# A new operation list for a gated convolution and a gated MLP on one core, with a small load moved to the front

## The chip, the cores and the metric

The kernel runs on one core of a Trainium2 chip. The metric is the device time in microseconds from the first to the last instruction of the program. The engines of the core are TensorE (PE, matmuls; its weight loads are shown apart as PEld), VectorE (DVE), ScalarE (ACT), GpSimd (POOL) and SyncE (SP), which only issues transfers here. They run side by side and wait for one another through semaphores.

## The reference

One block of 2048 positions (S) and 640 channels (D). A vector `c` gives six modulation rows. The first part is a layer norm, a short convolution of `k` over four positions, a product with `v`, a long convolution over the whole sequence through a Fourier transform, and a product with the normalised input. The second part is a gated MLP whose gate is mixed over positions. Batch 1, bfloat16:

```python
mod = (silu(c) @ w_mod).reshape(1, 6, 1, -1)           # sa, ca, ga, sb, cb, gb
h = layernorm(x) * (1 + ca) + sa                       # x is A_q
k_shift = sum over t of k_pad[:, t:t+S] * shift_k[:, 3-t]
kv = k_shift * v
y = irfft(rfft(kv, 2S) * rfft(ssm_k, 2S))[:S] + kv * ssm_D
x = x + ga * (h * y)
h = layernorm(x) * (1 + cb) + sb
z = gelu(h @ w_in)                                     # 640 -> 1728
z1, z2 = z[:, :864], layernorm(z[:, 864:])
g = w_sp @ z2 + b_sp[:, None]                          # 2048 x 2048 over positions
x = x + gb * ((z1 * g) @ w_out)
```

## The kernel before

The long convolution is done as two short transforms on TensorE. The channels are cut into five blocks (`u`) of 128. For each block, stage 1 turns the filter (XK) and the signal (XU) with a small table F1, `forward` turns the result with M2 in eight steps (`st`) of two frequencies, VectorE multiplies signal and filter, `inv` turns back with G2, and a last transform with the table E gives y. D is added to the filter's first tap, so that `kv * ssm_D` needs no work of its own.

The kernel records its first half (everything up to the mixing over positions) as about a thousand operations with their dependencies, and then issues them in the order of a written list. Each token names the engine (P, A, D, G, S for PE, ACT, DVE, POOL, SP) and the number of the operation:

```python
ORDER = """
D13 G96 D12 D122 D7 D8 D9 S14 A0 S5 A4 D95 D97 D104 A1 D110 D105 A2 G125 D6 S77 S78 ...
"""
def run(self, engines):
    order = [(x[0], int(x[1:])) for x in ORDER.split()]
    ...
    for e, i in order:
        o = self.ops[i]
        assert e in o["eng"] and done.issuperset(o["deps"]), (e, i)
        o["fn"](engines[e])
```

Within one engine the list is the order of execution; between engines only the dependencies order. An operation that may run on several engines is placed by its letter. These are the operations that the prediction speaks of:

```python
# loads, tables and D
nc.gpsimd.memset(D_col[:], 0.0)                        # at the end of GpSimd's set-up
op("SAG", "ldc", ... dma_start(c_bf, c), w=["c"])
op("A", "silut", activation(warm, warm, Silu)); op("A", "silu", activation(sc, c_bf, Silu))
op("A", "sint", activation(warm, warm, Sin), r=["silu"], w=["sint"])
op("SAG", "ldD", ... dma_start(D_col[0:P:16, :], d_fft), w=["D"])      # 8 x 80 elements
op("D", "addD", ... tensor_tensor(XK[:, x:y, 0], XK[:, x:y, 0], D_col[...], op=ALU.add), r=["D"], w=[XK])
op("A", "f1c", cosine(f1c, f1i), r=["f1a", "sint"])     # the table F1
op("D", "f1m", tensor_tensor(F1bd, f1c, gmask, op=ALU.mult), r=["f1c", "f1g"], w=["F1"])
# k and v by transposing loads, taps, kv to DRAM and back
op("S", "ldk", dma_start_transpose(kv[...], A_k or A_v))
op("P", "taps", 4 matmuls of 128x512 per quarter);  op("D", "tv", tensor_tensor(v, taps, v, op=ALU.mult))
op("SA", "kvw", dma_start(kv_scr, v));  op("SA", "ldX", dma_start(XU, kv_scr))
# one step of a block
op("P", "fwd", 6 matmuls);  op("D", "prod", tensor_tensor(T, pu, KH, op=ALU.mult))      # pu lies in PSUM
op("GD", "csum", tensor_tensor(W, T0, T1, op=ALU.add or ALU.subtract))                 # 2 inputs in SBUF
op("P", "inv", 6 or 12 matmuls); op("AD", "zc", copy(Z, pz))
# modulation and residual, per block and group of 4 x 128 positions
op("GD", "ghm", tensor_tensor(gh, gh, gca1 or gsa, op=ALU.mult or ALU.add))             # 2 inputs in SBUF
op("D", "ym", tensor_tensor(gh, gh, y, op=ALU.mult))                                     # y lies in PSUM
op("GD", "res", tensor_tensor(xt, xt, gh, op=ALU.add));  op("D", "ln2", bn_stats(st2, xt))
# second norm, per group; group 0 is flipped on TensorE, the others by a transposing move
op("G", "rstd2", rstd_from_var(...));  op("D", "nmr2", scalar_tensor_tensor(nmr2, mv2, -1, rstd2, ...))
op("DA", "zx", tensor_scalar(xn2, xt, mv2, rstd2, ...) or activation(...))
op("P", "hfl", transposes); op("AD", "hmod", ...)      # group 0
op("S", "turn", dma_start_transpose(hT, xn2)); op("DA", "hmod2", ...)                    # groups 1 to 3
op("P", "zz", 5 matmuls of 128x432); op("A", "gelu", ...)                                # 64 of these
op("P", "fill", k matmuls of the identity, results unused), k in FILLS
```

After the list the second half runs in program order: for each of 16 row blocks 32 matmuls that mix over positions (line 945 of the kernel before), a product on VectorE (948), a transposing move, and 14 matmuls with `w_out` (963).

Of the kernel before, what the change touches and what calls it, by code (L numbers as in the profile page):

```python
# [9 lines left out]
ACT = mybir.ActivationFunctionType  # L10
# [5 lines left out]
P = 128  # L16
# [17 lines left out]
FILLS = (4, 4, 4, 1, 2, 4, 2, 1, 4, 2, 2, )  # L34
# [6 lines left out]
D13 G96 D12 D122 D7 D8 D9 S14 A0 S5 A4 D95 D97 D104 A1 D110 D105 A2 G125 D6 S77 S78 D111 D81 A3 A106 A10 D11 A18 P1020  # L41
P1021 P1022 P140 P1023 P21 D116 D117 A107 S16 D82 P19 D98 A141 A118 A142 A119 D99 A100 D22 P143 A145 D144 S15 A101
A112 S17 A113 P146 A147 A148 G108 S29 S508 G109 D20 S27 D102 P1024 P25 D26 G120 A121 P23 D24 A28 P149 G114 A150 G115
P128 D129 D103 P1025 P131 D132 P134 A151 P158 G31 A159 D135 P162 A163 D512 P137 S30 G130 D138 D513 D514 D139 P164 A165
P156 A157 P154 A155 P36 D37 S79 P160 A161 P152 A153 P32 D33 G136 P168 P171 G43 A170 S80 D169 P34 D515 S83 A173 A172
P177 A179 P174 A176 D35 D178 P38 D39 D85 P166 A175 P194 D195 A167 G133 P220 A221 P180 G196 P204 A123 P222 A223 S509
D181 D205 P190 D191 P182 P214 G197 A516 G206 D183 P224 A225 P198 G55 A517 A199 S41 P184 P46 P226 A227 G207 P208 A209
S40 D215 G216 P48 D185 G186 G217 D518 S42 P200 G187 P192 A519 P230 A231 P218 G126 D201 D47 D520 P210 D211 S84 P244
A245 D49 P50 D51 A219 G521 D522 P240 D193 A241 P246 A247 D534 P232 A233 S550 P44 P228 A229 P250 A251 P242 A243 D535
D536 P551 A552 P238 A239 P248 A249 D45 S511 D527 D537 P234 A235 P553 P236 A237 S86 D538 D539 D88 P292 D528 P256 D257  # L50
P276 D277 G278 S510 A293 A529 G279 P212 A213 P294 A295 P252 A554 S52 D253 P188 A189 D523 P282 P202 P298 A299 D283 G258
G259 P266 A203 P254 A255 P296 A297 D267 D524 A530 P280 A281 S555 P556 P284 G268 G269 P558 D557 G597 D525 D526 S87 P316
A317 P310 P262 D531 P260 S53 S54 D263 D559 A311 P318 D285 S560 G532 A540 D541 D533 G576 P302 A303 P58 P286 A319 P60
A546 D287 D547 G288 D59 D578 P300 A301 G289 D61 P264 A542 A261 D543 D548 P312 A313 P320 A321 P304 A305 D544 P561 P56
D562 D579 D577 S89 P306 A307 D91 P322 A323 D545 G580 D57 P62 D63 P308 A309 P314 A315 P364 D549 D124 D582 P324 D325
P270 P338 D339 A365 P563 A265 G67 P366 P334 D335 A271 S584 P326 S64 A367 P368 G581 G583 P585 D564 D586 P358 P272 G340
G341 P290 G598 A369 G655 D359 G360 P587 S65 D588 A327 D273 P370 P342 G361 P348 D349 A291 D350 P589 D636 P72 A371 P376
D590 A377 D638 P274 A343 A275 S90 P388 A389 S66 P328 D329 P362 G603 D604 D657 G692 P372 A373 G330 D73 P591 D592 P390
G595 A391 P336 A337 P354 D355 P378 P392 A363 P70 A379 A393 P74 P374 P344 A375 P394 A395 D71 P384 D75 G351 D599 S92 D94
G600 D345 D634 D601 G602 S605 P68 D69 A385 P386 A387 P396 D397 P436 A437 P400 P352 A353 D401 P606 D607 G593 P382 A383  # L60
S76 G661 D635 P356 A357 P426 D427 G331 P440 A441 P608 P346 A347 D609 P380 A381 S565 G402 G403 S93 D637 P442 A443 D696
G697 G640 G641 P610 D611 P406 D407 P332 A333 P420 P438 A439 D421 P612 D613 P398 P404 A399 D594 P454 A455 D614 P460
P416 D693 P428 G422 G423 D616 A461 D417 P430 D431 A429 P466 A467 P566 A567 P410 A405 G659 P458 A459 P462 D694 A463
P418 S642 G619 D411 D639 D622 P444 A445 D618 D419 G432 P464 A465 G433 P643 D644 D623 D621 P448 A449 P450 A451 P424
A425 D620 P645 D646 P482 G662 P434 A435 P468 P647 P408 D483 S568 A409 P452 A453 D469 D648 G412 G413 P414 G484 G485
P502 D503 P492 D493 A415 P649 P470 A471 G656 P488 S738 P569 G624 P456 A457 P486 D489 A487 D650 P446 D617 P498 D499
G494 A447 G495 P496 A497 P478 D479 P490 A491 G504 G505 P472 P500 A501 P480 A481 G660 G658 S663 P664 P506 A570 A507
D473 D474 D475 P476 G698 A477 D665 P666 D667 P1026 P704 P668 G699 D615 G651 P706 D669 P1027 P670 A705 D707 D671 P702
P700 D701 A703 S571 P572 A573 D672 D674 G695 D673 P708 D709 D710 D713 D712 D711 D741 D740 G742 P724 D725 P717 D718
A127 P574 A575 P731 D743 A744 D745 P1028 P750 D714 P746 A747 G653 D732 D751 D719 P1029 P748 P754 D749 P752 A755 G677  # L70
D676 D753 P1030 P775 D716 S739 D715 D675 D757 D756 P800 D721 G652 D720 P772 D679 A776 G758 P806 D681 P782 D678 D759
A760 D723 D822 D823 D722 D680 A807 D761 D825 D824 G826 P768 D769 A801 P762 D763 A773 D827 D828 D829 D831 A783 D830
P802 P764 D726 D654 D730 D784 D682 D685 D683 A765 D684 G687 P766 A767 D728 P804 P770 A771 A805 P779 A780 A803 D729
P810 A811 P786 A787 D781 S832 P793 A794 P808 A809 P796 D691 A797 D690 D727 D626 A834 P789 A790 D836 D837 P814 P812
A835 D833 P862 G596 P838 A813 D688 G629 A815 A839 P880 D627 A881 P859 A860 A863 D777 P852 A853 P845 A846 D628 P874
A875 P848 A849 D890 D625 D888 D889 P876 A877 D686 D891 G892 D893 D894 D897 D896 D689 D895 P841 D631 A842 P868 A869
D733 P870 P878 D633 A871 S898 D630 D847 D737 D734 A900 P872 A879 D736 D632 D861 D956 D954 A873 P866 A901 P855 D843
A856 D840 A867 D844 D903 D774 D778 D902 D735 D955 D899 D957 D850 P914 P932 A933 P904 A905 A915 G958 D959 A960 D961
D962 D791 P934 D788 D795 D963 S964 A935 P918 A919 D792 P936 A937 D798 P907 A908 D851 D854 D799 D857 D858 D785 G816
D817 A820 P928 A929 D819 P911 A912 P925 D906 D818 A965 D967 A926 P921 A922 P942 P940 A941 D968 D969 D966 P970 P1002  # L80
P980 D864 A943 D916 A971 P938 A1003 D909 D913 D917 D865 A981 D920 P984 D930 D982 D910 D927 D931 P977 D923 A821 A939
A978 D979 A985 D986 P1004 A1005 D924 P987 A988 P991 A992 D989 G882 P998 G948 D949 D950 A952 P994 A995 D883 D953 P973
A886 A974 P1010 D972 D884 P1000 A999 A1001 A887 P1012 A1013 D885 D993 D951 A1011 D975 D976 P1008 P1006 A1007 D996 D997
P946 D983 D990 G1014 D1015 A947 D1017 P944 A945 A1019 D1018 A1009 D1016
"""


class Plan:


    def __init__(self):
        self.ops, self.touch = [], {}

    def op(self, eng, kind, fn, r=(), w=(), new=(), n=1):

# [28 lines left out]
def kernel(  # L124
# [20 lines left out]
    nc = tc.nc  # L145
    _, S, D = A_q.shape
# [58 lines left out]
    with ExitStack() as actx:  # L205
# [25 lines left out]
        op = plan.op  # L231
# [16 lines left out]
        def cosine(e, dst, turns64):  # L248

            e.activation(dst, turns64, ACT.Sin, bias=mpi[:], scale=TWO_PI / 64.0)  # L250
# [762 lines left out]
```

## Time and profile before

| | before |
|---|---|
| time, median of the runs | 334.87 us |
| profiled execution: span | 332.8 us |
| TensorE busy | 314.2 us (94%), 2596 instructions |
| VectorE busy | 218.8 us (66%), 466 |
| ScalarE busy | 147.0 us (44%), 257 |
| GpSimd busy | 93.5 us (28%), 120 |
| first matmul of the mixing | at 203.9 us |

One of the three runs before took 1839 us; the median leaves it out of account. In the slices of busy time (each digit a fortieth of the span, in tenths) one sees the two halves. VectorE is at 9 through the first half and at 2 or 3 in the second, TensorE is at 9 from the fourth slice on but for two slices at 8 and one at 5 at the end:

```profile
## 2 busy tenths in 40 slices
PE   6699999999999998699999899999999999999995
PEld 1366789778789897554455455555555555555553
DVE  6579999999999998989876783262223222233323
ACT  2476999896778756366667676000000000000010
POOL 2251733659489695551111111000000000000000
PEclk9699999999999999999999999999999999999999
```

PEclk is the clock that TensorE was granted. A matmul's busy time contains time in the pipeline, so a 9 of PE does not say that TensorE is the limit; which engine is, has to be read from the gaps and from the chain of waits. In the lists of operations, "out<-in" names the tiles, then come the shapes, the count and the busy time; `big` holds k and v (and later `w_in`), `X` the filter or signal, `gh` the modulated input and then the product with y, `xt` the running x, `Z` the inverse transform and later the normalised input, `s`, `sm`, `pu`, `pz` are tiles in PSUM.

### The profile page before, as it was taken

To read this page: it belongs to the slowest core of one execution; us is meant where nothing else is said; L and a number is where in the kernel's file an instruction comes from. 1 tells how busy PE (TensorE), PEld (TensorE's weight loads), DVE (VectorE), ACT (ScalarE), POOL (GpSimd) and SP (SyncE) were. 2 spreads that over 40 slices of the span, in tenths; PEclk is the share of its full clock that TensorE was granted. 3 is DMA by queue.
4 is the path that set the end of the run, shared out by engine and by line. 5 is a ranking of instruction groups with operands and counts; after the bars stand their busy time and mean duration, and the time that the engine had idled before them with its cause. 6 is when DMAs were issued, how large, how long until landed. Compare 5 with 4: busy or idle time off the path is not lost.

```text
span 332.8 us, 6423 instructions
## 1 busy us (share of the span) xinstructions
PE 314.2 (94%) x2596; PEld 206.7 (62%) x2603; DVE 218.8 (66%) x466; ACT 147.0 (44%) x257; POOL 93.5 (28%) x120
## 2 busy tenths in 40 slices
PE   6699999999999998699999899999999999999995
PEld 1366789778789897554455455555555555555553
DVE  6579999999999998989876783262223222233323
ACT  2476999896778756366667676000000000000010
POOL 2251733659489695551111111000000000000000
PEclk9699999999999999999999999999999999999999
DMA  7969999989969876004134991455557666422221
GB/s 128 204 129 249 243 299 239 234 186 194 197 185 156 272 131 231 2 1 79 21 60 81 175 226 51 91 118 116 116 131 131 135 83 150 110 49 47 49 47 59
DMA packets 128580, 44.99 MB, mean 135 GB/s; under 512 B 117704, under 2 KB 127784, under 8 KB 128552
## 3 DMA queue, kind: packets, MB, share of 16 engines
q1 hardware_dynamic: 127104, 44.33, 60.9%
q10 hardware_dynamic: 1448, 0.26, 0.4%
q8 instruction: 20, 0.33, 0.4%
q14 instruction: 8, 0.07, 0.1%
HBM read 16.11 MB, written 5.24 MB: 64 GB/s over the span
## 4 chain that ended last, share of the span: by engine, by line
PE 74%; DVE 14%; DMA 6%; issue 2%; ACT 2%; ACTq 0%; DVEq 0%
PE ps L945 28%; PE pu L240 15%; PE pz L240 12%; PE po L963 9%; PE sm L240 6%; DMA Z<-Z 4%; DVE Tf L456 3%; PE s L240 3%; DVE T L456 2%; DMA D_col<-in_A_ssm_D_dram 2%; DMA big<-in_A_k_dram 1%; DVE gh L648 1%; DVE W L465 1%; DVE st L569 1%; DVE big L542 1%
## 5 line engine op out<-in xcount | busy, mean ns | idle before, releaser
L945 PE MATMUL ps<-X,wT 128*128 128x432 bf16 x512 | 95.7, 346 | 0.0
L945 PEld LDWEIGHTS <-wT 128*128 128x128 bf16 x512 | 50.1, 98 | 42.2
L956 ACT COPY uT<-pt 128x896 bf16<-128x896 bf16 x1 | 0.9, 905 | 117.5 <-PE pt L955 117.5
L240 PEld LDWEIGHTS <-Z 128*128 128x128 bf16 x320 | 31.0, 98 | 29.4 <-ACT Z L858 1.7
L240 PE MATMUL pu<-X,M 128*128 128x128 bf16 (+1 forms) x480 | 46.2, 237 | 1.7 <-DVE Tf L456 1.1
L240 PEld LDWEIGHTS <-M 128*128 128x128 bf16 x480 | 37.5, 98 | 8.3 <-issue 3.0
L948 DVE SCALAR_TENSOR_TENSOR u<-ps,bcol,G 128x432 bf16<-128x432 f32 x18 | 12.0, 668 | 42.2 <-PE ps L945 42.2
L465 POOL TENSOR_TENSOR W<-Tf 128x256 bf16<-128x256 f32 x37 | 27.4, 760 | 27.7 <-DVE Tf L456 26.1
L243 ACT CAST X<-s 128x1024 bf16<-128x1024 f32 x32 | 32.8, 1024 | 4.5 <-PE s L240 4.4
L240 PE MATMUL pu<-big,Z 128*128 128x432 bf16 x160 | 32.3, 346 | 1.1 <-ACT X L883 1.1
L240 PE MATMUL pz<-big,Z 128*128 128x432 bf16 x160 | 32.3, 346 | 0.9 <-ACT X L883 0.7
L963 PE MATMUL po<-w_o,uT 128*128 128x320 bf16 (+1 forms) x224 | 32.8, 299 | 0.0
L948 DVE SCALAR_TENSOR_TENSOR u<-ps,bcol,M 128x432 bf16<-128x432 f32 x14 | 9.3, 667 | 30.9 <-PE ps L945 30.9
L240 PEld LDWEIGHTS <-G 128*128 128x128 bf16 x360 | 26.8, 98 | 2.2 <-DVE W L465 0.5
L963 PEld LDWEIGHTS <-uT 128*128 128x128 bf16 (+1 forms) x224 | 21.8, 98 | 9.8
L243 ACT CAST KH<-pu 128x512 bf16<-128x512 f32 x40 | 23.1, 596 | 9.1 <-PE pu L240 8.8
L456 DVE TENSOR_TENSOR Tf<-pu,KH 128x1024 f32<-128x1024 f32 x20 | 24.0, 1215 | 0.9 <-PE pu L240 0.8
L965 DVE TENSOR_TENSOR ot<-po,xt 128x320 bf16<-128x320 f32 x32 | 15.7, 492 | 13.4 <-PE po L963 13.4
L456 DVE TENSOR_TENSOR T<-pu,KH 128x1024 bf16<-128x1024 f32 x20 | 24.2, 1213 | 0.5 <-PE pu L240 0.5
L243 ACT CAST Z<-pz 128x512 bf16<-128x512 f32 x36 | 20.8, 592 | 6.3 <-PE pz L240 6.1
L240 PEld LDWEIGHTS <-X 128*128 128x128 bf16 x288 | 18.2, 99 | 8.3 <-DVE X L395 4.0
L240 PE MATMUL sm<-big,dg 128*128 128x512 bf16 (+3 forms) x73 | 21.4, 407 | 0.6 <-DVE big L542 0.2
(143 smaller groups left out, 425.8 us busy)
## 6 DMA issues: line engine op xcount, KB each, us to landing
wm<-in_w_mod_dram SPq DMA_DIRECT2D x6, 800.0 KB, 5.0
xt<-in_A_q_dram SPq DMA_DIRECT2D x4, 640.0 KB, 5.5
out_dram<-ot SPq DMA_DIRECT2D x16, 160.0 KB, 2.3
big<-in_B_w_in_dram SPq DMA_DIRECT2D x2, 1080.0 KB, 7.9
X<-in_A_ssm_k_dram SPq DMA_DIRECT2D x4, 512.0 KB, 6.2
kv_scr<-big SPq DMA_DIRECT2D x4, 512.0 KB, 4.1
X<-kv_scr SPq DMA_DIRECT2D x4, 512.0 KB, 4.8
w_o<-in_B_w_out_dram SPq DMA_DIRECT2D x6, 160.0 KB, 3.1
```

Source lines behind the costliest of these rows:

```text
L240: nc.tensor.matmul(o, lhsT=w, rhs=x, start=start, stop=stop)
L243: (e.copy if e is nc.scalar else e.tensor_copy)(dst, src)
L456: e.tensor_tensor(T_[:], tl[pu][:, :, :, None, :].to_broadcast([P, KP, 2, 2, DU]), tl[KH][:, :, None, :, :].to_broadcast([P, KP, 2, 2, DU] ...
L465: e.tensor_tensor(tl[W][:, :, o, :], T_[:, :, 0, o, :], T_[:, :, 1, 1 - o, :], op=ALU.add if o else ALU.subtract)
L542: e.tensor_tensor(vsl, tl[ps][:], vsl, op=ALU.mult)
L569: e.bn_stats(out=st[:, a, :], in_=xt[:, n, a * HS:(a + 1) * HS])
L648: lambda e, vec=vec, o=o: e.tensor_tensor(gvu, gvu, vec[:, None, d0:d0 + du].to_broadcast([P, TB, du]), op=o),
L945: nc.tensor.matmul(ps[:, :FC], lhsT=wTs[t][:, s_, :], rhs=tl["z2_%d" % (s_ // TB)][:, s_ % TB, fc * FC:(fc + 1) * FC], start=(s_ == 0), st ...
L948: nc.vector.scalar_tensor_tensor(u[:, sl], ps[:, :FC], bcol[:, t:t + 1], z1[t][:, sl], op0=ALU.add, op1=ALU.mult)
L956: nc.scalar.copy(uTs[t][:], pt[:])
L963: nc.tensor.matmul(ps[:, :HS], lhsT=uTs[t][:fsz[ft], ft, :], rhs=w_o[:fsz[ft], ft, h * HS:(h + 1) * HS], start=(ft == 0), stop=(ft == NFT ...
L965: nc.vector.tensor_tensor(ot[:, h * HS:(h + 1) * HS], ps[:, :HS], xt[:, t, h * HS:(h + 1) * HS], op=ALU.add)
```

## The change

The list of the first half was made anew by a planner that follows the program event by event, knows that VectorE and GpSimd shut each other out of memory in some operations, and counts the eight semaphores on which loads are counted. With it, D is loaded first, the extra Sin warm-up is dropped (Sin follows the Silu warm-up directly), the load of c and the silu move behind, and the fill matmuls go from 30 to 9.

```diff
-FILLS = (4, 4, 4, 1, 2, 4, 2, 1, 4, 2, 2, )
+FILLS = (4, 1, 4, )
 ORDER = """
-D13 G96 D12 D122 D7 D8 D9 S14 A0 S5 A4 D95 D97 D104 A1 D110 D105 A2 G125 D6 S77 S78 D111 D81 A3 ...
+A76 S3 D6 D94 D7 D12 D11 S4 A1 A9 D8 G95 D96 D115 S13 D103 D10 D116 A117 A118 D80 D5 P1019 ...
   (the whole list of 1031 tokens is replaced by one of 1022)
+        nc.gpsimd.memset(D_col[:], 0.0)      # now the fourth operation of GpSimd's set-up
-            op("A", "f1c", ..., r=["f1a", "sint"], w=["f1c"])
+            op("A", "f1c", ..., r=["f1a", "silut"], w=["f1c"])
   (the same for e2c and msin)
-        nc.gpsimd.memset(D_col[:], 0.0)
-        op("SAG", "ldc", ...)
+        op("SA", "ldc", ...)
-        op("A", "sint", lambda e: e.activation(warm[:], warm[:], ACT.Sin), r=["silu"], w=["sint"])
-        op("SAG", "ldD", ...)
-        op("SAG", "ldsk", ...)
+        op("S", "ldD", ...)
+        op("SA", "ldsk", ...)
```

The lists cannot be compared by the numbers, since one operation is gone; by name, the operations that are carried out by another engine than before are:

| operation | before | after |
|---|---|---|
| modulation of h (ghm) | 17 VectorE, 23 GpSimd | 13, 27 |
| residual addition (res) | 10 VectorE, 11 GpSimd | 14, 7 |
| partial sum of products (csum) | 3 VectorE, 37 GpSimd | 2, 38 |
| first normalisation (xn) | 13 VectorE, 3 ScalarE | 12, 4 |
| second normalisation (zx) | 13 VectorE, 3 ScalarE | 11, 5 |
| modulation behind the flips (hmod) | 5 VectorE, 5 ScalarE | 3, 7 |
| copy of G | 4 VectorE, 0 ScalarE | 2, 2 |
| copy of Z (zc), stage-1 copy (s1c) | 4 and 3 VectorE | 5 and 4 |
| normalisation of z (zn) | 10 VectorE, 6 ScalarE | 11, 5 |
| weights of the taps as diagonals | 4 GpSimd, 1 ScalarE | 4 GpSimd, 1 VectorE |
| D, c | issued on ScalarE's queue | on SyncE's |
| first half of the filter, one load of x, two of w_mod | on SyncE's queue | on ScalarE's |

In the new list the four residual additions that GpSimd made after the first projection matmul are VectorE's, and the last one that GpSimd makes stands ahead of the first product of the block that is flipped on TensorE.

## The prediction

> **What bounds the kernel now.** I read four views: the busy time by stage, the chain that ended last, the time line around the two places where that chain leaves TensorE, and the groups of VectorE operations with their shortest and mean durations.
>
> First the stages. I cut the span at the first filter product on VectorE (32.6 us), at the first matmul of the input projection (142.3) and at the first matmul of the spatial mixing (204). The columns are PE, PEld, DVE, ACT and POOL busy, clock, DMA share and GB/s.
>
> ```profile
> 0.00:32.60 32.60, 26.42 (x169) 15.12 (x171) 24.02 (x70) 18.12 (x39) 10.29 (x24) 0.90 0.88 175
> 32.60:142.30 109.70, 103.61 (x1356) 87.69 (x1363) 106.84 (x178) 84.17 (x138) 70.42 (x77) 1.00 0.84 197
> 142.30:204.00 61.70, 59.67 (x333) 31.82 (x332) 48.16 (x148) 41.90 (x78) 12.75 (x19) 1.00 0.45 93
> ```
>
> In the middle stage VectorE is busy 106.8 of 109.7 us: it is the limit there, and only 2.9 us of it are gaps. In the third, 320 projection matmuls at a spacing of 0.912/5 = 0.182 us (five take 0.91 us in the chain) make 58.4 us of 61.7, so TensorE is the limit. After 204 the chain is TensorE without gaps to the end (332.8 - 204 = 128.8 us), and the change does not touch it. What can move is the 32.6, the 109.7 and some 3 us of the 61.7.
>
> The chain shows why the first product waits until 32.6 (start, length, what):
>
> ```profile
> 0.72 3.92 DMA big<-in_A_k_dram
> 4.64 0.02 issue
> 4.66 0.02 ACTq L737
> 4.68 0.04 issue
> 4.72 5.32 DMA D_col<-in_A_ssm_D_dram
> 10.04 0.02 issue
> 10.06 0.20 DVE X L395
> 10.27 0.75 DVE F1bd L295
> 11.02 0.04 issue
> 11.06 0.59 PE pz L240 x2
> 11.65 0.43 PE pu L240 x2
> 12.07 0.43 PE s L240
> 12.50 3.41 PE sm L240 x8
> ```
>
> The 1.2 KB of D are issued on ScalarE's queue only when the first transposing load of k has landed at 4.64, although they do not need it: the two loads count on one semaphore. D lands at 10.04, VectorE adds it, builds the table F1, and TensorE begins its real work at 11.06. ScalarE stands behind the same issue: its table load starts at 6.03. From 11.06 the chain runs over TensorE to the first product, with eight taps at 3.41/8 = 0.43 us each.
>
> The second place is just ahead of the projection:
>
> ```profile
> 136.38 3.45 POOL L685 TENSOR_TENSOR xt<-xt,gh 128x512 bf16<-128x512 bf16 x3
> 136.44 1.11 DVE L800 SCALAR_TENSOR_TENSOR nmr<-mv,rstd 128x2 f32<-128x2 f32 x1
> ...
> 137.48 1.35 DVE L812 TENSOR_SCALAR Z<-xt,mv,rstd 128x640 bf16<-128x640 bf16 x1
> ...
> 138.75 1.24 DVE L685 TENSOR_TENSOR xt<-xt,gh 128x256 bf16<-128x256 bf16 x1
> ```
>
> Three GpSimd additions of 1.15 us lie side by side with three VectorE operations that elsewhere take 0.14, 0.43 and 0.29 us (the shortest of their groups). Each grows by about one GpSimd addition: 0.97 + 0.92 + 0.95 = 2.84 us, on the way to the first projection matmul. The same happens at 147.7 to 151.1.
>
> **What the Trainium skill says.** "SBUF — State Buffer", section "Who interferes with whom": a VectorE instruction with two SBUF inputs, or in a two-port mode, and a GpSimd instruction exclude each other, and the loser waits for the whole instruction. The trace agrees: the growth above is 0.92 to 0.97 us beside additions of 1.15 us, whereas the product, which has one input in PSUM, stays at 1.17 to 1.23 us in all 40. "DMA: Bandwidth & Descriptors", section "Issuing engines are not separate DMA queues": starting transfers on more engines saves only the time to start them. That is 0.45 us for c and 1.28 us for D on ScalarE's queue here, so moving two weight loads and one load of x there buys little. "TensorE: Matmul & The Clock Gate", section "What's actually happening": the array is slow until it has been busy for some 3.4 us. The trace agrees: taps of 512 columns at 0.43 us from 12.5, and 1.73/8 = 0.22 us from 17.74. Fewer dummy matmuls could therefore cost a little at the start.
>
> **The change part by part.**
>
> *Start.* D goes first on SyncE's queue. It needs the clearing of D_col, which moves ahead of three other GpSimd operations, so it is issued near 1.4. With the 5.3 us from issue to landing of before, it is there at about 6.7. The first half of the filter is issued on ScalarE's queue at 0.7 and with its 4.3 us lands earlier. ScalarE has then one issue of about 0.7 us (two take 1.32) ahead of its table load (1.28), and no silu, which moves behind: the cosine is done near 3.5 instead of 8.4. F1 (0.84) is done before D is there. So the first stage-1 matmul starts near 7.1 instead of 11.06: 4 us earlier. Not all of it arrives. k is issued third, near 3.2, and v after the second half of the filter and of k. The second half of v is then issued no earlier than before (near 9, against 7.8), and the product needs v: kv goes to DRAM, is read back (3.8 us until the write has landed, 3.8 to read), transformed, and multiplied. I put the second write of kv, 20.23 before, at 17.2: the taps of the last two blocks finish near 16 and their product with v near 17. That makes the first product 3.0 us earlier, at 29.6. VectorE's own work ahead of it is the same to 0.1 us (4 stage-1 copies instead of 3, a diagonal of weights and one more negation, against 2 copies of G fewer), about 24 us, and would allow it.
>
> *Middle stage.* The counts of VectorE operations between the first product and the first projection matmul change by: 4 fewer modulations of h (0.41 each when undisturbed), 1 fewer partial sum (0.57), 1 fewer normalisation of x (0.43), 1 fewer modulation behind the flips (0.41), 1 more copy of Z (0.68), 4 more statistics (0.35), 2 more aggregations (0.21). Sum: -3.05 + 0.68 + 1.40 + 0.42 = -0.55 us. GpSimd takes 4 modulations (1.18) and one sum (0.76) more, 5.5 us, on 70.4 busy of 109.7. It has the room.
>
> The exclusion is the larger term. VectorE lost in this stage, mean minus undisturbed times count: modulations 9.0 - 17 x 0.41 = 2.0, sums 3 x (1.13 - 0.57) = 1.7, normalisations 13 x 0.06 = 0.8, and the three above 2.84. Together 7.3 us. In the new list the last GpSimd addition of the residual stands ahead of the first product of the last flipped stage; between it and the projection GpSimd has only the 0.9 us of the reciprocal root, and the four additions that lay in the third stage are VectorE's. So I count the 2.84 as gone, and leave the other 4.5, since more GpSimd work can also hit VectorE more often.
>
> *Third stage.* Before, TensorE waits 0.7 and 0.2 us for the second group and 1.1 us for the fourth; flips before the first groups wait 1.7. The new list has ten projections (9.1 us) between the last normalisation of the second group and its first use, against a transposing move of 4.9 to 7.0 us and 1.4 us of modulation: the wait goes, 0.9 gained. For the fourth group it has eight (7.3 us) where there were nine (8.2), against 7.0 + 1.4 = 8.4: the wait grows by about 0.9. I put down 0.5 lost, since nothing protects the order at the end of this stage.
>
> *Fill matmuls.* 30 become 9. They sit in TensorE's waits; 7 of the early 19 lie behind 11.06, in the chain with 0.43, 0.43 and at most 0.9 us. This is inside the 3.0 above.
>
> Sum: 3.0 + 0.5 + 2.8 - 0.5 = 5.8 us. A new order of a thousand operations brings gaps of its own where the old one had only 2.9 us on VectorE; I take 0.9 off. 334.87 - 4.9 = 330.0 us.
>
> **The rivals.** *The load of v takes the place of D.* For it: v is issued behind more transfers than before, and both halves have to be there before the whole of the first block is written. Then the start gives 1 us or less, and the time is 332. Against it: TensorE was only ready for the last taps at 17.6, long after v could have landed. *VectorE is the limit, and the exclusion only moves.* For it: the operations handed to GpSimd are just the ones with two SBUF inputs, and GpSimd grows by 5.5 us. Then the 2.8 us reappear as longer modulations and sums, and the time is 332 to 333. Against it: the new list was made with the exclusion in view, and the seven additions that hurt most are placed elsewhere. *More of the 7.3 us goes.* If half of the other 4.5 us is saved too, and the start gives its full 4 us, the time is 327. *A cold or starved transition.* The fill matmuls around 130 to 142 are gone but for four; if the projection starts at half clock, some 16 matmuls cost 0.18 us more each, 3 us, and the time is 333. The clock of that stage was 1.00 throughout, with work between.
>
> **Range and chances.** The terms are uncertain by about 1.5 us (start), 2 us (exclusion), 1.5 us (third stage) and 2 us (gaps of the new list), together 3.5 us, which is not quite symmetric since an order is easier to spoil than to perfect. Eight in ten: 326.3 to 334.5. Two per cent faster is 328.2, about half a spread below the middle: 0.29. Two per cent slower is 341.6: 0.04. The rest, 0.67, lies within.
>
> **What would show it.** D's load issued before 1.6 and landed before 7; the first stage-1 matmul near 7; the first product near 29.6; the first projection near 136.5, with the reciprocal-root, normalisation and residual operations ahead of it at 0.14, 0.43 and 0.3 us; the first mixing matmul near 199; and from there 128.8 us as before. I am wrong if the first product stays beyond 31.5 (v, not D, sets it), if the middle stage stays at 109 us with VectorE as busy as now (the exclusion moved), or if TensorE shows a gap of 2 us or more in the third stage.

## The result, and the profile after

The new kernel takes 326.4 us (median of 4 runs, 325.6 to 327.2) against 334.66 us for the kernel before beside it: a ratio of 0.9755, 95% interval 0.9722 to 0.9789. Measured again among the experiments, the same kernel came to 0.9805 (0.9772 to 0.9838). The two intervals overlap, and the two values of one kernel differ by 0.005; differences up to that between ratios from different measurements are therefore not read below.

The busy time by stage, cut as in the prediction at the first filter product, the first projection matmul and the first mixing matmul (columns as there):

```profile
0.00:31.20 31.20, 24.04 (x161) 15.12 (x163) 23.60 (x71) 18.74 (x34) 9.10 (x22) 0.95 0.99 205
31.20:136.30 105.10, 100.25 (x1344) 86.63 (x1349) 99.75 (x175) 83.76 (x139) 75.20 (x84) 1.00 0.81 199
136.30:195.40 59.10, 59.10 (x333) 31.79 (x332) 46.33 (x143) 43.33 (x81) 9.25 (x16) 1.00 0.49 97
195.40:324.10 128.70, 124.69 (x744) 72.17 (x742) 39.97 (x75) 2.53 (x4) 0.00 (x0) 1.00 0.43 93
```

The start gave 1.4 us (32.6 to 31.2), the middle 4.6 (109.7 to 105.1), the third stage 2.4 (61.5 to 59.1) and the rest 0.3: together 8.7 us between the two profiled executions. In the middle VectorE (third busy column) is busy 99.75 us instead of 106.84, 7.1 us less, but its gaps grew from 2.9 to 5.4 us. In the third stage TensorE is busy for all of the 59.10 us: nothing is left to gain there by order alone.

At the start, TensorE's time line shows its waits in brackets:

```profile
6.19 0.61 PE L240 MATMUL pz<-F1bd,X 128*128 128x256 bf16 x2 [0.86 <-DVE X L396]
...
21.16 1.04 PE L240 MATMUL s<-F1bd,X 128*128 128x256 bf16 x4 [2.34 <-DVE X L396]
```

D came as predicted (issued at 1.38), and the first stage-1 matmul starts at 6.19 instead of 11.06. But at 18.8 TensorE stops for 2.34 us, for a filter tile. The chain of waits (start, length, what) says why:

```profile
10.50 4.70 SPq L511
...
15.24 5.61 DMA X<-in_A_ssm_k_dram
...
20.87 0.24 DVE X L396
...
21.16 1.04 PE s L240 x4
```

Line 511 is the transposing load of k for the second block. Its issue alone holds SyncE's queue for 4.70 us, and the second block's filter, which is needed first, stands behind it. The pause costs more than its 2.34 us: from 21.17 to 24.58 TensorE's granted clock is 0.50. The four matmuls at 21.16 take 0.83 us until the next starts, where the same four take 0.44 in the run xk_early below, which has no such stretch; with the 20 matmuls behind them, 3.39 us against 1.78, 1.6 us lost.

The transition into the projection, on VectorE's time line:

```profile
133.21 0.15 DVE L799 SCALAR_TENSOR_TENSOR nmr<-mv,rstd 128x2 f32<-128x2 f32 x1
133.28 0.44 DVE L811 TENSOR_SCALAR Z<-xt,mv,rstd 128x640 bf16<-128x640 bf16 x1
```

Where the same operations took 1.11 and 1.35 us before, they now have their undisturbed lengths, and both residual additions of 128x256 take 0.29 us, where one took 1.24. In the row of slices of the kernel before, TensorE's 17th digit (133.1 to 141.4 us) is a 6: that is this transition, and the text there passes over it.

### The profile page after: what moved, and what is told of

The parts are those of the page before. It is cut to its first block, busy times and chain, and to the rows that moved or that the text cites. A ratio compares the mean times of both kernels' runs of the same rounds, so it can differ in the third digit from the quotient of the medians.

```text
span 324.1 us, 6365 instructions
## 1 busy us (share of the span) xinstructions
PE 308.1 (95%) x2574; PEld 205.7 (63%) x2582; DVE 209.6 (65%) x463; ACT 148.4 (46%) x255; POOL 93.6 (29%) x121
## 4 chain that ended last, share of the span: by engine, by line
PE 74%; DVE 12%; DMA 7%; SPq 4%; issue 1%; ACT 1%; POOL 0%; DVEq 0%; POOLq 0%
PE ps L944 29%; PE pu L240 15%; PE pz L240 13%; PE po L962 9%; DMA ZT<-Z 5%; PE sm L240 5%; SPq L511 3%; PE s L240 3%; DVE Tf L457 2%; DVE T L457 2%; DMA X<-in_A_ssm_k_dram 2%; DVE st L570 2%; DVE big L543 1%; DVE X L243 1%; PE sm L823 0%
## 5 line engine op out<-in xcount | busy, mean ns | idle before, releaser
L240 PE MATMUL pu<-X,M 128*128 128x128 bf16 (+1 forms) x480 | 47.1, 240 | 1.5 <-DVE T L457 0.9
L240 PEld LDWEIGHTS <-Z 128*128 128x128 bf16 x320 | 31.1, 98 | 26.6 <-DVE Z L832 0.4
L240 PE MATMUL pz<-big,Z 128*128 128x432 bf16 x160 | 32.6, 346 | 0.0
L888 DVE BATCH_NORM_STATS2 stz<-X 128x6 f32<-128x432 bf16 x32 | 18.2, 594 | 7.1 <-ACT X L882 7.1
```

Of the source, the lines that this page charges most:

```text
L240: nc.tensor.matmul(o, lhsT=w, rhs=x, start=start, stop=stop)
L888: op("D", "stz", lambda e, i=i, n=n, fc=fc: e.bn_stats(out=stz[:, n, fc, :], in_=tl[z2][:, i, fc * FC:(fc + 1) * FC]), r=[(z2, (i, fc))], ...
```

## The experiments

My theory from the two traces: the middle gains because VectorE is no longer shut out by GpSimd (A), the third stage has an order of its own that fits (B), and the start is held by SyncE's queue and not by D any more (C). The rivals: it is the order and not the division of work (against A); the stages' gains depend on one another and do not add up (against all three). First all runs in one table: length of the start, the middle and the third stage in the profiled execution (us), and the ratio to the kernel before.

| kernel | start | middle | third | ratio (95% interval) |
|---|---|---|---|---|
| before | 32.6 | 109.7 | 61.5 | 1 |
| new | 31.2 | 105.1 | 59.1 | 0.9755 (0.9722 to 0.9789) |
| new, again (after_again) | 30.6 | 105.1 | 59.1 | 0.9805 (0.9772 to 0.9838) |
| engines_back | 30.6 | 114.6 | 60.7 | 1.0089 (1.0059 to 1.0119) |
| res_moved | 32.4 | 107.5 | 60.4 | 0.9885 (0.9852 to 0.9919) |
| pool_adds | 30.8 | 106.3 | 59.1 | 0.9804 (0.9765 to 0.9843) |
| tail_old | 31.7 | 106.2 | 60.2 | 0.9842 (0.9801 to 0.9882) |
| start_old | 30.6 | 111.8 | 59.1 | 0.9981 (0.9955 to 1.0008) |
| d_first | 31.1 | 109.6 | 61.5 | 0.9983 (0.9966 to 0.9999) |
| xk_early | 30.0 | 105.6 | 59.1 | 0.9795 (0.9744 to 0.9846) |
| kv_early | 31.2 | 105.0 | 59.1 | 0.9767 (0.9738 to 0.9796) |
| kv_read_first | 33.9 | 106.6 | 59.1 | 0.9870 (0.9839 to 0.9901) |
| kv_late_k1 | 28.3 | 112.8 | 59.1 | 0.9953 (0.9932 to 0.9973) |
| three_edits | 30.9 | 107.5 | 61.2 | 0.9898 (0.9874 to 0.9923) |

In the edits shown, only the tokens that change and their neighbours stand, "..." marks what is left out, and text in brackets stands for whole parts of a list. A token is the engine's letter and the operation's number.

### The new kernel again: after_again

No edit.

> The new kernel unchanged, as the measure for the three beside it. All theories: 0.975 of the kernel before, as in its first comparison; its first product near 31.2 us, first projection matmul near 136.3, first mixing matmul near 195.4. If it differs from 0.975 by more than 0.004, differences below that between kernels measured at different times are not to be read.

Measured: 0.9805, marks 30.6, 135.66 and 194.75. The start of the same program moves by 0.6 us from one execution to another; middle and third stage repeat to 0.1 us. A start's length is therefore not read where it differs by less than 1 us, and start_old below shows that even 2 us can come from one execution's state.

### Division or order: engines_back

```diff
 new list, same order; 31 tokens change their engine to that of the kernel before, e.g.
-... G581 ... G576 ... G577 G578 ... D597 G349 ...
+... D581 ... D576 ... D577 D578 ... G597 D349 ...
```

> The new list in its order, but the 31 modulations, partial sums and residual additions that changed between VectorE and GpSimd are given back to the engine of the kernel before (VectorE gets 14 from GpSimd... counted: 11 modulations, 3 sums, 2 additions to VectorE; 7 modulations, 2 sums, 6 additions to GpSimd). Theory 'the division of the work is what counts': the exclusion comes back, VectorE is busy 5 us or more longer between first product and first projection, and 4 us or more of the gain are lost (330 us or more). Theory 'the order is what counts': VectorE has only its 4 more modulations and 1 more sum less 4 additions, about 1 us, and the time is within 1.5 us of the new kernel. A list that was made event by event for one division may lose more than either by waits of its own; then the gaps of VectorE, and not its busy time, grow.

Measured: 1.0089 (1.0059 to 1.0119), the whole gain lost and more. The middle takes 114.6 us. VectorE's groups of that stage, first with the engines given back, then in the new kernel (group xcount | busy us, mean ns | idle before):

```profile
L649 DVE TENSOR_TENSOR gh<-gh,gca_bf 128x512 bf16<-128x512 bf16 x10 | 6.7, 668 | 0.1
...
L649 DVE TENSOR_TENSOR gh<-gh,gsa_bf 128x512 bf16<-128x512 bf16 x7 | 4.5, 643 | 0.1
...
L686 DVE TENSOR_TENSOR xt<-xt,gh 128x512 bf16<-128x512 bf16 x4 | 2.6, 660 | 0.1
...
L799 DVE SCALAR_TENSOR_TENSOR nmr<-mv,rstd 128x2 f32<-128x2 f32 x1 | 0.9, 881 | 0.0
```

```profile
L649 DVE TENSOR_TENSOR gh<-gh,gca_bf 128x512 bf16<-128x512 bf16 x8 | 3.4, 420 | 0.1
L649 DVE TENSOR_TENSOR gh<-gh,gsa_bf 128x512 bf16<-128x512 bf16 x4 | 2.2, 557 | 0.0
L686 DVE TENSOR_TENSOR xt<-xt,gh 128x512 bf16<-128x512 bf16 x4 | 1.7, 418 | 0.0
...
L799 DVE SCALAR_TENSOR_TENSOR nmr<-mv,rstd 128x2 f32<-128x2 f32 x1 | 0.2, 154 | 0.0
```

Read the means: the same kind of operation takes mostly 0.42 us (0.56 in one row) in the new kernel and 0.64 to 0.67 with the engines given back. These rows, the partial sums (2 of 415 ns, 3 of 542 with the engines given back) and the first normalisation (12 of 436 ns, 12 of 479) sum to 13.0 us in the new kernel and 21.4 here. Six more operations are worth 6 x 0.42 = 2.5 us of the 8.4; the other 5.9 us are the same operations made longer. VectorE's gaps are nearly the same (114.55 - 108.53 = 6.0 us against 105.06 - 99.70 = 5.4). So in this order nearly the whole loss is VectorE's busy time, and most of that is the exclusion: theory A. What the run does not show is that this division would do it in another order, with other GpSimd operations beside those of VectorE.

### The six late additions alone: res_moved

```diff
 list of the kernel before
-... G653 ... G677 ... G652 ... G687 ... G596 ... G629 ...
+... D653 ... D677 ... D652 ... D687 ... D596 ... D629 ...
```

> The kernel before with its old list; only the six residual additions that GpSimd makes after the reciprocal root of the first group, near the first projection matmul, are VectorE's. Theory of the prediction (those additions cost 2.84 us on the way to the first projection matmul): reciprocal-root product, normalisation and addition at 0.14, 0.43 and 0.3 us, VectorE has 6 additions of 0.3 to 0.45 us more, first projection matmul 0.5 to 1.5 us earlier than 142.3, and the third stage loses its repetition at 148 to 151; the whole 1 to 2 us faster. Rival (the gain is in the division of all modulations, sums and additions and in the order, not in these six): within 1 us of the kernel before.

Measured: 0.9885 (0.9852 to 0.9919), 3.7 us, more than either theory gave. VectorE's time line at the transition:

```profile
136.26 0.16 DVE L800 SCALAR_TENSOR_TENSOR nmr<-mv,rstd 128x2 f32<-128x2 f32 x1
136.34 0.44 DVE L812 TENSOR_SCALAR Z<-xt,mv,rstd 128x640 bf16<-128x640 bf16 x1
136.69 0.62 DVE L685 TENSOR_TENSOR xt<-xt,gh 128x256 bf16<-128x256 bf16 x2
```

The first projection matmul comes 2.4 us earlier (139.89 against 142.27) although VectorE does more: six letters in the old list (0.2 of the 2.4 us is a shorter start). The third stage becomes 1.1 us shorter too (61.5 to 60.4), since the same collision at 147 to 151 us is gone (there the next factor takes 0.16 us instead of 1.04). The 2.84 us that the prediction counted at this place were about right.

### GpSimd additions put into the new kernel: pool_adds

```diff
 new list, behind the reciprocal root of the first group; three additions whose results nobody uses
-... G741 D742 ...
+... G741 G1022 G1023 G1024 D742 ...
```

> The new kernel with three additions of 128x512 on GpSimd behind the first reciprocal root, whose result nobody reads. If the exclusion of VectorE and GpSimd cost the time there, the nmr and the normalisation beside them grow from 0.15 and 0.44 us to about 1.1 and 1.3, the first projection comes 1.5 us later (1.0 to 2.0), and the time is about 327.9 us. If it does not, they stay and the time stays at 326.4.

Measured: the middle is 1.2 us longer, the ratio 0.9804 cannot be told from the new kernel's. VectorE beside the additions, and the second and third of the additions on GpSimd:

```profile
133.53 0.77 DVE L799 SCALAR_TENSOR_TENSOR nmr<-mv,rstd 128x2 f32<-128x2 f32 x1
134.22 0.44 DVE L811 TENSOR_SCALAR Z<-xt,mv,rstd 128x640 bf16<-128x640 bf16 x1
```

```profile
134.35 1.19 POOL L918 TENSOR_TENSOR sc_rep<-ident 128x512 bf16<-128x512 bf16 x1
135.62 1.04 POOL L918 TENSOR_TENSOR sc_rep<-ident 128x512 bf16<-128x512 bf16 x1
```

The first VectorE operation grew by 0.62 us, the second not at all. In the kernel before both had grown. The Trainium skill ("SBUF — State Buffer", section "Who interferes with whom") says that the one that issues first gets the shared ports and the other blocks. The trace agrees: the first added addition ends at 134.28, VectorE's normalisation had started at 134.22, the second addition starts only at 134.35, and now it is the addition that is longer, 1.19 us against 1.04 for the first and third. The added ones write one tile in turn, and each starts 0.08 us after the one ahead has ended; the real ones of the kernel before start 0.04 us before the one ahead ends, which leaves no such gap. So this run tests the exclusion in one of its two operations. Of the 1.2 us, 0.62 arise here; 0.5 come from another place, a wait for a load of x at 45 us. The 1.5 us expected here were too high; the next run shows the real additions.

### The old third stage behind the new middle: tail_old

```diff
-[new list from the first projection matmul on]
+[the same operations in the order and on the engines of the kernel before]
```

> The new list up to the first projection matmul, everything behind it in the old order, with four residual additions back on GpSimd. If the third stage gains by its own order, as the traces show (61.7 against 59.1 us), the time is 326.4 + 2.5 = 328.9 us and TensorE shows the waits of before again (0.9 us at the second group, 1.1 at the fourth). If the third stage is shorter only because what precedes it has left it less to do, 326.4 to 327.

Measured: 0.9842 (0.9801 to 0.9882). The third stage takes 60.2 us, 1.1 us longer than in the new kernel. The first projection matmul comes at 137.85, 1.6 to 2.2 us later. Two of the old additions run on GpSimd from 133.40 for 2.26 us, and VectorE beside them has

```profile
133.69 0.88 DVE L799 SCALAR_TENSOR_TENSOR nmr<-mv,rstd 128x2 f32<-128x2 f32 x1
134.49 1.35 DVE L811 TENSOR_SCALAR Z<-xt,mv,rstd 128x640 bf16<-128x640 bf16 x1
```

0.73 and 0.91 us more than in the new kernel, 1.64 us together; 1.1 of them are left at the first projection matmul (middle 106.2 against 105.1), the rest of its delay is the start. Here the real additions lengthen both operations, as in the kernel before. The old order is worth another 1.1 us in the third stage; start, middle and third stage make up the 2.7 us between the spans of 326.8 and 324.1. Of the waits of before, those for the second group came back (0.6 and 0.2 us), the 1.1 us for the fourth did not.

### The old start ahead of the new rest: start_old

```diff
-[new list up to the first filter product]
+[the same operations in the order and on the engines of the kernel before]
```

> The new list with everything ahead of the first product in the old order (D behind k, old fills), the rest in the new order. If the three stages add up as the two traces show them (start 1.4 us, middle 4.6, third 2.5), this loses the 1.4 us of the start: 327.8 us, first product near 32.6. If an earlier start is worth the 3.0 us of the prediction and VectorE's new gaps of 5.3 us in the middle stage come from an early start, about 329.5. If the middle absorbs the start, 326.4.

Measured: 0.9981 (0.9955 to 1.0008), so at most half a per cent of the gain is left, with single runs from 330.5 to 336.9 us; the profiled execution, at 332.3, is 2 us under the median. All my expectations missed: the first product came at 30.6, as early as in the new kernel, and the middle became 6.7 us longer. The old start was itself 2 us faster here than in the kernel before (32.6): the first stage-1 matmul came at 10.09 instead of 11.06, since D landed and F1 was built sooner, and TensorE's matmuls were at half rate until 14.1 instead of 16.9. So a start that is 1.4 us shorter in one execution is not shown to be the new list's doing. The middle by the busy time, and VectorE's waits in it (us in total, times, longest):

```profile
30.60:142.40 111.80, 102.71 (x1348) 87.59 (x1354) 100.00 (x176) 85.31 (x139) 74.02 (x82) 0.98 0.83 193
```

```profile
DVE gh L666 <- PE sm L240: 3.2, 4, 1.8
DVE T L457 <- PE pu L240: 2.0, 3, 1.5
DVE Z L832 <- PE sm L823: 1.8, 1, 1.8
DVE st L570 <- DMA xt<-in_A_q_dram: 1.2, 1, 1.2
```

VectorE has the new, short 100.0 us of work, but 11.8 us of gaps instead of 5.4. Its operations stand in the same order in both traces, so that they can be compared one by one: the delay against the new kernel grows by 1.6 and 0.8 us at the second and third product, by 1.2 at a load of x, by 0.5 at a filter's load, by 1.5 at a product with y near 113 us and by 1.3 at the first modulation behind the flips, near 141 us. The last has a cause that the trace shows: TensorE's granted clock is 0.50 from 136.6 to 140.2, where it is 1.00 in the new kernel. The same matmuls ahead of the flips, here and in the new kernel:

```profile
136.91 1.51 PE L240 MATMUL sm<-wm,sc_rep 128*128 128x320 bf16 x5 [0.31 <-DVE gh L728]
```

```profile
132.11 0.85 PE L240 MATMUL sm<-wm,sc_rep 128*128 128x320 bf16 x5 [0.31 <-DVE gh L728]
```

The lesson is in the pair of numbers: the same division of work, the same order of the middle, and by the median all of the gain given back in waits. What in the state at the first product brings about the other waits, the loads under way or the work already done, was not separated. The time of the first product alone says little.

### D first, alone: d_first

```diff
 list of the kernel before; D_col cleared as early as in the new kernel
-D13 G96 ... S14 A0 S5 A4 D95 ...
+S4 D13 G96 ... S14 A0 S5 D95 ...
```

> The kernel before with its old list, only D is loaded first on SyncE's queue (and cleared earlier). Theory of the prediction (D holds up the start): D landed near 6.7, first stage-1 matmul 3 to 4 us earlier, first product about 3 us earlier than 32.6. Theory from the new trace (k*v through DRAM sets the first product): first stage-1 matmul earlier by 2 us or more, first product earlier by 1.5 us or less, whole time within 1.5 us of the kernel before.

Measured: 0.9983 (0.9966 to 0.9999), about 0.6 us (1.1 at most); the first product 1.5 us earlier, in the profiled execution. The first stage-1 matmul starts at 9.33 instead of 11.06: behind D, the filter's own load (5.20 to 8.69) holds it, which the new list avoids by issuing that load at 0.72 on ScalarE's queue. Moving D alone is worth little in the end.

### The filter of the second block ahead of its k: xk_early

```diff
 new list
-... A147 S28 A146 ... A160 S82 D84 ...
+... A147 S82 S28 A146 ... A160 D84 ...
```

> The new kernel with the load of the second block's filter issued ahead of the second block's k instead of behind it, nothing else. If the 2.3 us that TensorE waits for this load near 20 us set the first product, it comes 1 to 2 us earlier and the time is 325 us. If the way of kv through DRAM sets it, TensorE waits later instead and the time stays within 0.4 us of 326.4.

Measured: 0.9795 (0.9744 to 0.9846), not to be told from the new kernel. The wait of 2.34 us for the filter is gone, and the first product comes at 30.0, 0.6 to 1.2 us earlier. What takes its place is in the chain of waits:

```profile
10.99 6.81 SPq L511
...
17.94 3.94 DMA kv_scr<-big
...
21.93 3.13 DMA X<-kv_scr
...
25.11 0.39 PE pz L240 x2
```

The way of k*v through DRAM (write 3.94 us, read 3.13) now sets the first product, and the write waits for the same transposing load, whose issue here takes 6.81 us.

### The write of k*v out of that queue: kv_early

```diff
 as xk_early, and
-... P153 A164 ... D514 S27 ...
+... P153 A27 A164 ... D514 ...
```

> The new list, with the second block's filter loaded ahead of the second block's k, and the second write of k*v issued on ScalarE's queue as soon as the product is there, instead of behind the 4.7 us issue of that k on SyncE's queue. Theory 'the way of k*v through DRAM sets the first product': write issued near 15.2 instead of 16.0 (and instead of 17.9 with the filter alone moved), the signal read back about 1 to 2 us earlier, first product at 29 us (31.2 in the new kernel, 30.0 with the filter alone moved), and 1 to 2 us off the whole. Rival 'the middle stage is bound by VectorE and its order': first product earlier, but the first projection matmul stays within 0.5 us of 136.3 and the time with it.

Measured: 0.9767 (0.9738 to 0.9796) beside 0.9805 for the new kernel on the same chip; the intervals overlap, a gain is not shown. The write was issued at 14.74, a little earlier than expected, but took 5.2 us to land (19.94), where it took 3.94 in xk_early; the issue of the second block's v on SyncE's queue (17.23, 2.70 us) ended at the same moment. The read followed at 20.07 and took 4.67 us. The first product stayed at 31.2.

### The read ahead of v, and of k: kv_read_first and kv_late_k1

```diff
 kv_read_first: as kv_early, and
-... S29 S78 D36 S79 ...
+... S78 S79 S29 ... D36 P33 ...
 kv_late_k1: as kv_early, and k and v of the second block, with their taps, behind the reads
-... S82 S28 A146 ... P35 S29 S78 D36 S79 P31 ...
+... S82 A146 ... S78 S79 S28 S29 ... P35 D36 ... P31 D32 P33 ... D34 P37 ...
```

> As the run with the second write of k*v on ScalarE's queue and the filter moved ahead, and the reading back of k*v also stands ahead of the second block's v on SyncE's queue. Theory 'SyncE's queue, held by transposing loads of the second block, set the reading back': the two reads are issued near 17.5 to 19.5 us instead of 20.1, land near 22 to 23, first product near 29 instead of 31.2, the whole 0.5 to 1.5 us under the new kernel. Rival 'the middle stage absorbs it': first product earlier but first projection matmul within 0.5 us of 136, ratio 0.975 to 0.981 as before.

> As that run, but the second block's k, too, is loaded behind the reading back of k*v, and the second block's taps stand behind the first two products of the first block. Same theory: the reads are issued as soon as the write has landed, near 18 us, first product near 26 us, five before the new kernel. Does it arrive at the end? If VectorE's busy time (23.6 us before the first product, 99.7 after it) is what bounds the first half, the first projection matmul comes at most 2 us earlier, since 23.6 of the 31.2 us are its work already and the 2 x 0.7 us of taps' products move behind the first product. If the late k and v of the second block make new waits, the gain is lost again.

Measured: 0.9870 (0.9839 to 0.9901) and 0.9953 (0.9932 to 0.9973), both worse than the new kernel. In the first, SyncE's queue is free for the reads from 17.6 us, but they are issued only at 20.53: the write, issued at 15.42, needs 5.0 us to land. So the landing of the write set the reading back, and in kv_early it would have held it to the same 19.94 us without the queue: the theory of the queue fails. Besides, VectorE waits 2.1 us for v and TensorE 3.1 us for the taps' product, ahead of the first product (33.9). In the second, with the transposing loads of the second block behind the reads, the reads are issued at 18.95, 4.1 us after the write; the first product comes at 28.3, nearly 3 us before the new kernel, and the middle is 7.7 us longer:

```profile
28.30:141.10 112.80, 105.64 (x1367) 88.75 (x1366) 102.57 (x179) 83.88 (x138) 75.26 (x84) 0.99 0.84 196
```

That is like start_old. Part of it is work put off: the work that VectorE did not do before 28.3 (VectorE is busy 20.96 us there instead of 23.60) is done later (2.8 us more in the middle), VectorE's gaps in the middle are 10.2 us instead of 5.4, and the whole delay has arisen by 52 us. For part of that time, from 23.1 to 30.0, TensorE's granted clock is 0.50; what this adds was not separated. I did not find a version that is shown to beat the new kernel.

### Three edits of the old list: three_edits

```diff
 [old list up to the first projection matmul]   [new list from there]
-[D on ScalarE's queue, as eleventh]
+[D on SyncE's queue, as first]
-[late residual additions, behind the first reciprocal root, on GpSimd]
+[the same on VectorE]
```

> The old list up to the first projection matmul, with two edits in it: D loaded first on SyncE's queue, and the late residual additions of GpSimd given to VectorE; from the first projection matmul on the new list. If the three gains add up: first product near 31.1 us (1.5 earlier, as with D first alone), first projection matmul near 138.4 (another 2.4 earlier, as with the additions moved alone), third stage 60 us or less (60.2 with the old middle and the new start's counterpart, 59.1 in the new kernel), ratio 0.982 to 0.985 to the kernel before. What is then left to the new kernel (0.9755 and 0.9805 in two comparisons) is the new division and order of the middle stage, 1 to 2 us. If the gains do not add up (as the new start alone, which gave 2 us and lost them in the middle), the ratio is 0.988 or more. If it reaches 0.980 or less, the new order of the middle stage is worth nothing beyond these.

Measured: 0.9898 (0.9874 to 0.9923). Start and middle add up as expected (30.9, first projection matmul at 138.35), but the third stage is 61.2 us, hardly better than the old 61.5, where the new kernel has 59.1 with the same list. TensorE's longest waits near and in it:

```profile
PE sm L823 <- ACT Z L809: 1.7, 2, 1.5
```

The flips of the next group wait 1.5 us for the normalisation on ScalarE, which waits 1.81 us for VectorE's factor; VectorE is making that group's residual additions and statistics until 141.7. Together with tail_old this shows that the 2.4 us of the third stage need both its new order (which behind the old middle gives 0.3) and what the new middle has done ahead of it (VectorE has four more statistics there).

## Why the prediction was right or wrong

330.0 us were predicted, with a range from 326.3 to 334.5; 326.4 came out, inside it by a tenth. The direction and the places were right; one path and four sizes were not, and they partly cancel: the first projection matmul came at 136.3 where 136.5 was predicted, with a start 1.6 us too long and a middle shorter than reckoned. That agreement is luck.

*Start: 3.0 predicted, 1.4 measured.* D, the table F1 and the first stage-1 matmul came as worked out (6.19 against 7.1). The failing step is the path from there on, which runs through v and the second write of k*v to the first product. That write was issued at 15.96, earlier than the 17.2 reckoned, though its landing took 5.6 us where 3.8 were reckoned. What TensorE waited for was a load that the path does not contain, the second block's filter, behind the 4.70 us issue of a transposing load on SyncE's queue: 2.34 us of waiting, and 1.6 us of half rate behind it. The rival "1 us or less because of the loads" had the right kind of cause and the wrong load. In xk_early, without that wait, k*v through DRAM is the next limit, at 30.0. And since the old start also came to 30.6 in start_old, even the 1.4 us are one pair of executions.

*Exclusion: 2.8 predicted, 5 to 6 measured.* VectorE's busy time in the middle fell by 7.1 us. Fewer operations are about 2 of it and not 0.55: one modulation of h, one modulation behind the flips and one product with y (0.41 + 0.41 + 0.68) stand behind the first projection matmul that the prediction counted ahead of it. The other 5 are operations that became shorter; adding up their lengths one by one, without their overlap, gives 5.9. The step that failed is "leave the other 4.5": I took as gone only the three operations at the transition. In the new kernel the modulations lose 8 x 0.01 + 4 x 0.15 = 0.7 us against the undisturbed 0.41, the normalisations 0.1, the sums (0.42 each, which makes their loss before 2.1 and not 1.7), the residual additions and the transition next to nothing. In return two small operations of the first norm, which the prediction does not name, now lie beside GpSimd and take 0.94 and 0.64 us where they took 0.12 and 0.16: 1.3 us that did only move. engines_back shows how much hangs on the division of the work, res_moved and tail_old that the loss at the transition was real (2.2 and 1.1 us of the middle). I had the evidence for more, since the change said that the planner knew the exclusion; the reason I gave for caution, that GpSimd takes more work (75.2 us against 70.4), weighed little, because most of what lies beside it now keeps its length.

*Gaps: 0.9 taken off, 2.5 measured.* VectorE's gaps grew from 2.9 to 5.4 us, mostly waits for TensorE (1.7 us instead of 0.6 ahead of the product with y). The sign was right, the size too small.

*Third stage: 0.5 lost predicted, 2.4 gained.* The wait of the second group went, as predicted. The step that failed is the fourth group: "eight projections (7.3 us) against 7.0 + 1.4". The eight stood there, but the transposing move was faster. Its time from issue to landing (least, median, most), before and after:

```profile
DMA to landing us min/median/max: 4.9/6.0/7.0
```

```profile
DMA to landing us min/median/max: 4.9/5.0/5.1
```

5.1 + 1.4 = 6.5 us fit into 7.3. I had taken the slowest move of the old list as if it were a property of the move. The slowest takes 7.0 to 7.2 us in all four executions with the old list ahead of the projection (before, d_first, res_moved, three_edits) and at most 5.2 in the ten with the new one, tail_old with its old third stage among them. So it goes with what stands ahead of the projection; by what, was not tried.

*The rest.* In both profiled executions of the new kernel TensorE kept its clock at the transition (1.00 in the middle and the third stage), with 9 fill matmuls as with 30. So the rival of a cold transition does not explain its time; but it is real: the clock fell to 0.50 ahead of the first projection in start_old and in kv_read_first (134.6 to 138.0), and the delay at the first modulation behind the flips grew by 1.3 and 1.2 us. Of "the exclusion only moves", 1.3 us came true. "More of the 7.3 goes", at 327, named the middle rightly but got there with a full start, which did not come.

Summed with the measured terms, start, fewer operations, exclusion, gaps, third stage and the rest: 1.4 + 2.0 + 5.1 - 2.5 + 2.4 + 0.3 = 8.7 us, the difference of the two spans.

## What to carry to other kernels

If the limiting engine's operations have means well above their shortest instance, add up that excess for all groups, not only where the chain of waits passes: here it was 7 of 107 us, and a new list that chooses engine and order with the collisions in view brought 5 to 6 of them back, net of a new loss of 1.3 us. Count what stands on either side of a stage's mark again when the list changes. Six letters in the old list, at the one place where the chain showed the collision, bought 3.7 us; read that place first. Do not value a stage by its end mark: a start that is 3 us shorter because work was put off cost 7.7 us later (kv_late_k1), and parts of two lists put together gave less than their gains would sum to (start_old, three_edits).

## What was unexpected of the hardware

The issue of one transposing load on SyncE's queue took 4.70 us in the new kernel, 6.81 in xk_early, 6.37 in kv_early and 6.44 in kv_read_first, where loads of half its size took 1.3 to 1.7 and others of its size 2.7 to 3.8; everything behind it on the queue waited. The Trainium skill ("DMA: Bandwidth & Descriptors", section "Issuing engines are not separate DMA queues") calls the time to start a transfer usually small beside the transfer; here it is nearly as long as the whole load of the filter behind it (5.61 us), so the order on the queue, and which queue, mattered after all. The long ones came behind four large loads (half of k, both halves of v, and x) issued within the 5.1 us before. In kv_late_k1 the same load, issued at 20.83 without them, took 2.58 us, and in the kernel before, behind half of k and both halves of v, 2.37; so their number may matter, but that was not tried by itself.

TensorE's clock fell at places that its pauses do not explain. After 2.34 us without work it ran at half rate in the new kernel and after 2.50 us in kv_early, and at full rate in xk_early after 2.73. In start_old it fell at 136.6, where the longest pause of the 7 us before was 0.45 us. Every stretch at clock 0.50 that the traces record lasts 3.4 or 6.8 us, but for one at the very end of each program. In the kernel before it is 6.8 us, and TensorE's work is at half rate from 11.06 to about 16.9: 5.8 us, not the 3.4 that the prediction took the trace to agree with. The chain of waits of kv_early, to be read against the 0.39 us for the same two matmuls in xk_early:

```profile
24.79 0.61 PE pz L240 x2
...
26.68 1.68 PE sm L240 x4
28.35 0.22 PE pz L240 x2
```

Four taps take 1.68 us there and 0.86 once it is fast again. What decides when the clock falls is open.
